# Rows of an attention stage turned by VectorE in 32x32 blocks and written from SP's queue, in place of TensorE transposes

## The chip, the cores and the metric

The kernel runs on one core of a Trainium2 chip. The time is the device time of that core in microseconds, taken as the median of several executions. The profile is one further execution, recorded by the hardware profiler.

## The reference

A linear attention with decay, for 4 sequences (b), 8 heads, 768 positions and 64 features per head, feeds a mixture of 8 experts. Cut to what matters:

```python
for b in range(nb):                      # blocks of positions, state carried on
    intra = (q_b @ k_b^T * Dmask) @ v_b  # Dmask = lam ** (i - j), lower triangle
    inter = (q_b * lam ** (i + 1)) @ kv_state
    out_b = intra + inter
    kv_state = lam ** block * kv_state + (k_b * lam ** (block - 1 - i))^T @ v_b
x = out as (4, 768, 512)                 # heads side by side
logits = x @ w_gate                      # 8 experts
e = argmax(logits), or the expert of the token before if sigmoid(x @ w_local) >= 0.5
out = softmax(logits)[e] * (relu(x @ w1[e]) @ w2[e])
```

Everything is in float32. Which tokens an expert gets is known only at run time.

## The kernel before

**Stages.** The kernel has an attention stage, a routing calculation woven into it, and an expert stage. The attention stage has 24 steps (`NS`), one for each block of 128 positions (`c`, 6 of them) of each sequence (`b`, 4 of them); `ORDER` goes through the four sequences first. The expert stage gathers rows of tokens from a DRAM tensor `x_dram` (3072 rows of 512 features), turns them, multiplies them with the weights of one expert at a time, and scatters the results.

**One step.** Step `s` takes an input tile `inp` of 1 MB: q and k with features on the partitions, v and k with positions on the partitions, each 128 x 512. TensorE computes the scores of the step to come (`scores`, line 200 or 208), the part that comes from the state (`from_state`, 235), the mixing of the values by the scores (`mix`, 248), the update of the state (`update`, 262) and the rows of the step before (`rows_of`, 272). VectorE multiplies the scores with the decay mask (212, two instructions) and adds to the state (265). ScalarE copies the result from PSUM to `xc` (251), decays the state (239) and copies the turned rows (277). GpSimd multiplies q and k with powers of lambda (`prepare`, 177 and 180), three steps ahead.

**The result `xc`.** It has features on the partitions: `xc[p, d, b, i]` is feature 128 d + p of position i. The gating product (`gates`, 286, every fourth step) reads it so. The expert stage needs whole rows of tokens in DRAM. So `rows_of(s)` turns the four 128 x 128 pieces with TensorE into one PSUM bank, ScalarE copies the bank into a tile `xn` (four buffers), and one DMA from ScalarE's queue writes 128 rows of 2 KB to `x_dram`; the last three of these writes go from SP's queue.

**Scores.** For steps in the list `WIDE` (3, 4 and 5) the scores are computed in 8 products with 128 keys each (line 200). In all other steps the keys are taken in halves of 64, in 16 products (line 208), and where a half lies behind all its first queries, those queries are left out.

**Order and queues.** In the attention stage the order on TensorE, VectorE, SP and GpSimd is the order of the program (`manual_schedule`); ScalarE's is chosen by the scheduler. SP's queue carries the input loads: the load of step s + 5 is issued at the top of step s, into one of six buffers, and waits until step s - 1 has been done with its buffer. Weights of the first two experts follow from step 16 on, on the same queue. Routing work stands in a table `extras` by step: constants (`constants_2` to `constants_6`, steps 6 to 10) are converted from integers or from float32 to what the routing needs, by VectorE, and from step 9 on the routing itself runs there.

**Weights.** `w1` is reordered on the host (`swapped`) so that its rows stand in the order of the features in `x_dram`.

Of the kernel before, what the change touches and what calls it, by code (L numbers as in the profile page):

```python
# [8 lines left out]
F32 = mybir.dt.float32  # L9
# [14 lines left out]
P = 128  # L24
B, H, S, DH = 4, 8, 768, 64
A = H // 2
DM = H * DH
E, F = 8, 1024
DT, FT = DM // P, F // P
N = B * S  # L30
NT = N // P
NC = S // P
ORDER = [(b, c) for c in range(NC) for b in range(B)]
# [5 lines left out]
PARTS = [(0, 8), (8, NA), (NA, NT)]  # L39
LOADS = 6  # L40
QUARTERS = [16, 17, 18, 19]
WIDE = [3, 4, 5]
WARM = 10
KA = -(-(NA * P - E * (P - 1)) // P)

# [2 lines left out]
HP = P // 2  # L48
QP = P // 4
# [5 lines left out]
G = G2 + E  # L55
# [9 lines left out]
def kernel(  # L65
# [9 lines left out]
    nc = tc.nc  # L75
# [7 lines left out]
    x_dram = dram.tile([N, DM], F32, name="x_dram")  # L83
# [18 lines left out]
    ident = const.tile([P, P], F32, name="ident")  # L102
# [4 lines left out]
    pg = ctx.enter_context(tc.tile_pool(name="pg", bufs=1, space=PSUM))  # L107
    x_ctx = ExitStack()
    load = x_ctx.enter_context(tc.tile_pool(name="load", bufs=LOADS))
    att = x_ctx.enter_context(tc.tile_pool(name="att", bufs=2))  # L110
# [11 lines left out]
    def piece(k):  # L122
        return spare[:, A * P * k:A * P * k + A * P]
# [35 lines left out]
    NS = len(ORDER)  # L159
# [4 lines left out]
    xc = att.tile([P, A, B, P], F32, name="xc", bufs=1)  # L164
# [21 lines left out]
    def scores(s):  # L186
# [8 lines left out]

        if s in WIDE:
            for a in range(A):
                for u in range(2):
                    rows = slice(DH * u, DH * u + DH)
                    nc.tensor.matmul(ps[u][:, a], lhsT=kt[rows, a], rhs=qt[rows, a],  # L200
                                     start=True, stop=True, skip_group_check=True)
        for a in range(A if s not in WIDE else 0):
            for j in range(2):
# [63 lines left out]
                nc.vector.tensor_copy(kv, pk)  # L267

    def rows_of(s):
        px = pg.tile([P, DM], F32, name="pk1")  # L270
        for a in range(A):
            nc.tensor.transpose(px[:, P * a:P * a + P], xc[:, a, ORDER[s][0]], ident)  # L272
        if s + 1 < NS:
            xn = att.tile([P, DM], F32, name="xn", bufs=4)
        else:
            xn = xlast
        nc.scalar.copy(xn, px)


        queue = nc.scalar if s + 3 < NS else nc.sync  # L280
        queue.dma_start(out=x_dram[P * s:P * s + P, :], in_=xn)

    def gates(k):

# [18 lines left out]
    count = const.tile([P, G + 1], F32, name="count")  # L303
    countb = const.tile([P, P], BF16, name="countb")
    whole = const.tile([P, G + 1], F32, name="whole")
    identb = const.tile([P, P], BF16, name="identb")
    onesb = const.tile([P, P], BF16, name="onesb")
    beforeb = const.tile([P, P], BF16, name="beforeb")
    dupb = const.tile([P, P], BF16, name="dupb")
    upper = const.tile([P, 1], F32, name="upper")  # L310
    dupq = const.tile([P, P], BF16, name="dupq")
# [4 lines left out]
    parts = route.tile([P, NT, 5], BF16, name="parts")  # L316
    ints = [piece(5 + i).bitcast(I32) for i in range(2)]
# [12 lines left out]
            nc.gpsimd.memset(t[:, :, 0:1], 0.0)  # L330

    def constants_2():
        nc.vector.tensor_copy(count, ints[0][:, :G + 1])
        nc.vector.tensor_copy(whole, ints[0][:, P:P + G + 1])
        nc.vector.tensor_copy(identb, ident)
        nc.vector.tensor_scalar(down, count[:, :E], -1.0, float(E), ALU.mult, ALU.add)

    def constants_3():
        nc.vector.tensor_copy(countb, ints[0][:, :P])

    def constants_4():
        nc.vector.tensor_copy(beforeb, ints[1][:, P:2 * P].bitcast(F32))
        nc.vector.tensor_copy(parts[:, :, 0], whole[:, 1:NT + 1])
        nc.vector.tensor_copy(parts[:, :, 1], ints[0][:, 2 * P:2 * P + NT])

    def constants_5():
        for half in range(2):
            nc.vector.tensor_copy(dupb[:, HP * half:HP * half + HP], ident[:, :HP])
        nc.vector.tensor_reduce(upper, ident[:, HP:], axis=AX.X, op=ALU.add)

    def constants_6():
        for k in range(4):
            nc.vector.tensor_copy(dupq[:, QP * k:QP * k + QP], ident[:, :QP])
        row = ints[0][:, 2 * P:2 * P + 1]
        nc.vector.tensor_scalar(row, row, P - QP, None, ALU.bitwise_and)
        nc.vector.tensor_scalar(fourth, row, 1.0 / QP, None, ALU.mult)
# [342 lines left out]
    xlast = moe.tile([P, DM], F32, name="xlast", bufs=1)  # L699
# [66 lines left out]
    def number(k, n):  # L766
# [3 lines left out]

    extras = {
        (6, 1): constants_2, (7, 1): constants_3, (8, 1): constants_4, (9, 1): constants_5, (10, 1): constants_6,
        (9, 0): lambda: fresh_experts(0), (10, 0): lambda: along_sequences(0), (11, 0): lambda: experts_of(0),
        (12, 0): lambda: ranks(0), (13, 0): lambda: fresh_experts(1), (14, 0): lambda: (along_sequences(1), masks(0)),
# [10 lines left out]
    with tc.manual_schedule(engines={PE, DVE, SP, POOL}):  # L785
# [16 lines left out]
        for s in range(NS):  # L802
# [4 lines left out]
            if s in QUARTERS:  # L807
                j = QUARTERS.index(s)
# [23 lines left out]
            if s == 1:  # L832
                query_powers(1)
                prepare(4)
                rows_of(0)
# [4 lines left out]
            if s > 1:  # L840
                rows_of(s - 1)
# [34 lines left out]
        moved(xtt[1], xq, (0, 1))  # L876
        hidden(0, 0, 0)
        rows_of(NS - 1)
        weights(1)
        gates(NC - 1)  # L880
# [452 lines left out]
```

## Time and profile before

| | |
|---|---|
| runs | 453.72 us median of 3 (451.68 to 459.57) |
| profiled execution | 449.21 us, span 447.5 us |
| granted TensorE clock | 0.995 |
| busy in the span | TensorE 433.0 us, VectorE 278.4, ScalarE 202.0, GpSimd 109.2 |
| attention stage | to about 103 us |
| four row transposes of a step | 0.59 us on the chain |
| `xn` copy, ScalarE | 586 ns each |
| 32x32 transposes of 128 x 512 on VectorE (expert stage) | 700 ns each |
| row write, issue to landing | 7.4 us (median of 21 DMAs, 256 KB each) |
| input load, issue to landing | 8.8 us (median of 15 DMAs, 1 MB each) |

A line of the chain of waits gives a start, a length and what ran; the numbers behind x are instructions. A line of the table of stages gives the stretch, its length, and then the busy time and the instructions of TensorE, its weight loads, VectorE, ScalarE and GpSimd, the granted clock, the busy share of the 16 DMA engines and GB/s. A line of the waits gives who waited for whom, the sum, how often, and the longest. A line of the DMA queues gives packets, MB and the share of 16 engines' time; a line of DMA issues gives the size and the median time from issue to landing.

### The profile page before, as it was taken

The numbers are of one execution on the slowest core, as the hardware profiler recorded it, in microseconds if no ns is written. First come the engines' busy times: TensorE is split into PE (matmuls) and PEld (weight loads), VectorE is DVE, ScalarE is ACT, GpSimd is POOL, SyncE is SP. The second block draws the span as 40 slices with busy tenths as digits, with TensorE's granted clock in tenths as the row PEclk, the third lists the DMA queues.
The fourth block names the chain that finished last, engine by engine and source line by source line (L and its number), as shares of the span: only waits on it lengthen the run. The fifth ranks groups of instructions, "written<-read, shape, count | busy, mean of one in ns | idle before, by whom it ended". The sixth has DMA issues, their size and how long they took to land.

```text
span 447.5 us, 10529 instructions
## 1 busy us (share of the span) xinstructions
PE 433.0 (97%) x4202; PEld 359.3 (80%) x4202; DVE 278.4 (62%) x562; ACT 202.0 (45%) x594; POOL 109.2 (24%) x120
## 2 busy tenths in 40 slices
PE   7999999999999999999999999999999999999993
PEld 6877877768667866979686999667899999898982
DVE  5546867881419949866473796100487888878661
ACT  2355656546453205553434447451445455556110
POOL 4476656231100041204120301210102011020101
PEclk9999999999999999999999999999999999999997
DMA  8999989988899889999995699997153838380101
GB/s 267 409 420 392 323 305 320 354 305 325 275 403 365 325 277 378 398 395 404 394 399 214 180 403 372 346 368 254 41 212 107 313 97 287 140 280 4 53 3 51
DMA packets 42575, 124.85 MB, mean 279 GB/s; under 512 B 3148, under 2 KB 3148, under 8 KB 40592
## 3 DMA queue, kind: packets, MB, share of 16 engines
q1 hardware_dynamic: 34976, 104.62, 64.0%
q0 software_dynamic: 4368, 13.90, 8.8%
q10 hardware_dynamic: 3168, 5.51, 3.3%
q8 instruction: 37, 0.61, 0.5%
q14 instruction: 26, 0.21, 0.1%
HBM read 124.02 MB, written 12.91 MB: 306 GB/s over the span
## 4 chain that ended last, share of the span: by engine, by line
PE 82%; DMA 7%; issue 6%; DVE 3%; POOLq 0%; POOL 0%
PE ps L731 13%; PE pk L737 12%; PE ps L956 12%; PE pk L961 11%; DMA out_dram<-y,sidxp 6%; PE po L248 6%; PE po L956 5%; PE pl L961 4%; PE ps L208 4%; PE pk L272 3%; PE po L235 2%; PE pk L262 2%; PE pr L1117 2%; PE pr L1095 2%; PE pl L286 1%
## 5 line engine op out<-in xcount | busy, mean ns | idle before, releaser
L731 PEld LDWEIGHTS ps<-xt,w 128*128 128x128 f32 x512 | 58.2, 192 | 3.0 <-issue 2.3
L731 PE MATMUL ps<-xt,w 128*128 128x128 f32 x512 | 59.1, 276 | 0.3 <-DVE xt L713 0.3
L737 PE MATMUL pk<-w,h 128*128 128x512 f32 x128 | 56.5, 593 | 0.0
L737 PEld LDWEIGHTS pk<-w,h 128*128 128x128 f32 x128 | 23.6, 190 | 26.3 <-issue 25.6
L746 POOL DMA_INDIRECT out_dram<-y,sidx x14 | 14.0, 1002 | 105.8 <-DVE y L763 46.5
L212 DVE TENSOR_TENSOR sm<-ps,mask 128x512 f32<-128x512 f32 x46 | 29.6, 685 | 16.1 <-PE ps L208 6.6
L703 POOL DMA_INDIRECT xg<-x_dram,gidx x25 | 25.8, 1032 | 55.2 <-DVE lg L717 24.6
L724 ACT COPY xp<-xlast 32x128 f32<-32x128 f32 x128 | 37.8, 295 | 1.7
L733 ACT ACTIVATE h<-ps 128x512 f32<-128x512 f32 x16 | 9.6, 597 | 57.6 <-PE ps L731 57.6
L724 ACT COPY xp<-lg 32x128 f32<-32x128 f32 x112 | 33.0, 295 | 2.6
L763 DVE TENSOR_SCALAR y<-pk,gate 128x512 f32<-128x512 f32 x8 | 6.0, 745 | 42.1 <-PE pk L737 40.0
L956 PEld LDWEIGHTS ps<-xp,w 128*128 128x128 f32 x256 | 30.5, 192 | 1.7 <-issue 1.3
L177 POOL TENSOR_TENSOR qd<-inp,lamq 128x512 f32<-128x512 f32 x20 | 25.6, 1278 | 25.1 <-PE po L235 15.8
L956 PE MATMUL ps<-xp,w 128*128 128x128 f32 x256 | 31.3, 275 | 0.0
L956 PE MATMUL ps<-xs,s 128*128 128x128 f32 x256 | 31.2, 275 | 0.0
L248 PE MATMUL po<-sm,inp 128*64 128x128 f32 x384 | 28.1, 280 | 2.5 <-DVE sm L212 1.4
L961 PE MATMUL pk<-w,h 128*128 128x256 f32 x128 | 30.5, 381 | 0.0
L961 PE MATMUL pk<-s,hsum 128*128 128x256 f32 x128 | 30.3, 380 | 0.0
L956 PEld LDWEIGHTS ps<-xs,s 128*128 128x128 f32 x256 | 29.9, 192 | 0.0
L248 PEld LDWEIGHTS po<-sm,inp 128*64 128x64 f32 x384 | 21.3, 136 | 10.2 <-issue 7.7
L961 PEld LDWEIGHTS pk<-s,hsum 128*128 128x128 f32 x128 | 23.9, 190 | 3.3 <-DVE s L1044 0.2
L961 PEld LDWEIGHTS pk<-w,h 128*128 128x128 f32 x128 | 23.5, 190 | 3.4 <-issue 0.6
(280 smaller groups left out, 793.9 us busy)
## 6 DMA issues: line engine op xcount, KB each, us to landing
w<-in_w_dram SPq DMA_DIRECT2D x43, 2048.0 KB, 11.8
inp<-in_qkv_dram SPq DMA_DIRECT2D x15, 1024.0 KB, 8.8
x_dram<-xn ACTq DMA_DIRECT2D x21, 256.0 KB, 7.4
inp<-in_qkv_dram SPq DMA_DIRECT2D x10, 512.0 KB, 7.9
inp<-in_qkv_dram SPq DMA_DIRECT2D x4, 768.0 KB, 6.9
w<-in_w_dram SPq DMA_DIRECT2D x4, 512.0 KB, 9.3
x_dram<-xn SPq DMA_DIRECT2D x2, 256.0 KB, 8.6
xg<-x_dram,gidx POOLq DMA_INDIRECT x25, 6.3
```

Source lines behind the costliest of these rows:

```text
L177: nc.gpsimd.tensor_tensor(qd, x[:, 0].rearrange("p (a i) -> p a i", i=P), lamq, ALU.mult)
L208: nc.tensor.matmul(ps[u][half, a, first:], lhsT=kt[rows, a, half], rhs=qt[rows, a, first:], start=True, stop=True, skip_group_check=True)
L212: nc.vector.tensor_tensor(sm[:, u], ps[u], mask[:, u], ALU.mult)
L248: nc.tensor.matmul(head(a, u), lhsT=vn[:, a, u], rhs=sm[:, u, a], start=(not c and a < 2), stop=True, skip_group_check=True)
L272: nc.tensor.transpose(px[:, P * a:P * a + P], xc[:, a, ORDER[s][0]], ident)
L703: nc.gpsimd.indirect_dma_start(out=xg, out_offset=None, in_=x_dram[:n, :], in_offset=bass.IndirectOffsetOnAxis(ap=gidx[i][:, j:j + 1], axi ...
L724: copy(xt[QP * j:QP * j + QP, :, QP * k:QP * k + QP], blocks[QP * k:QP * k + QP, :, j])
L731: nc.tensor.matmul(ph[:, j], lhsT=w1t[w][:, d, P * f:P * f + P], rhs=xtt[i][:, d], start=(d == 0), stop=(d == DT - 1))
L737: nc.tensor.matmul(pys[i], lhsT=hq[f // 4, i][:, f % 4], rhs=w2t[w][:, f], start=(f == 0), stop=(f == FT - 1))
L746: apart(nc.gpsimd.indirect_dma_start(out=out, out_offset=bass.IndirectOffsetOnAxis(ap=sidx[i][:, j:j + 1], axis=0), in_=y, in_offset=None, ...
L956: nc.tensor.matmul(to[:, m], lhsT=a[:, k, P * m:P * m + P], rhs=b[:, k], start=(new and not m and not k), stop=(k == 1), skip_group_check= ...
L961: nc.tensor.matmul(to, lhsT=a[:, f], rhs=b[:, f], start=(new and not f), stop=(f == FT // 2 - 1), skip_group_check=True)
```

## The change

In 14 of the 24 steps (`BY_BLOCKS`: 0 to 10, 12, 14 and 22) `rows_of` uses one VectorE instruction that transposes every 32 x 32 block of the step's part of `xc`. Partition 32 j + r of the tile `xn` then holds, for position 32 i + r of the block (i from 0 to 3), the 128 features with (feature mod 128) from 32 j to 32 j + 31. Four DMAs from SP's queue, one for each i, write this to 32 rows each, in pieces of 128 features (512 bytes). In the other ten steps TensorE still turns the rows, and ScalarE's copy brings the features into the same new order. The order of the features in `x_dram` is now (j, d, c) instead of (d, j, c), and `w1` is reordered on the host to match.

Thirteen conversions of constants move from VectorE to ScalarE. Steps 8 and 11 join the steps with 128-key scores.

```diff
-WIDE = [3, 4, 5]
+WIDE = [3, 4, 5, 8, 11]
+BY_BLOCKS = [*range(11), 12, 14, 22]
...
     def rows_of(s):
-        px = pg.tile([P, DM], F32, name="pk1")
-        for a in range(A):
-            nc.tensor.transpose(px[:, P * a:P * a + P], xc[:, a, ORDER[s][0]], ident)
-        if s + 1 < NS:
-            xn = att.tile([P, DM], F32, name="xn", bufs=4)
+        b = ORDER[s][0]
+        xn = att.tile([P, DM], F32, name="xn", bufs=4) if s + 1 < NS else xlast
+        if s in BY_BLOCKS:
+            nc.vector.transpose(xn.rearrange("p (i d c) -> p i d c", i=4, c=QP),
+                                xc[:, :, b].rearrange("p d (i c) -> p i d c", c=QP))
+            for i in range(4):
+                rows = x_dram[P * s + QP * i:P * s + QP * i + QP, :]
+                nc.sync.dma_start(out=rows.rearrange("a (j m) -> j a m", j=4), in_=xn[:, P * i:P * i + P])
         else:
-            xn = xlast
-        nc.scalar.copy(xn, px)
-        queue = nc.scalar if s + 3 < NS else nc.sync
-        queue.dma_start(out=x_dram[P * s:P * s + P, :], in_=xn)
+            px = pg.tile([P, DM], F32, name="pk1")
+            for d in range(DT):
+                nc.tensor.transpose(px[:, P * d:P * d + P], xc[:, d, b], ident)
+            nc.scalar.copy(xn.rearrange("p (j d c) -> p j d c", j=4, c=QP), px.rearrange("p (d j c) -> p j d c", j=4, c=QP))
+            queue = nc.scalar if s + 3 < NS else nc.sync
+            queue.dma_start(out=x_dram[P * s:P * s + P, :], in_=xn)
...
     def constants_2():
-        nc.vector.tensor_copy(count, ints[0][:, :G + 1])
-        nc.vector.tensor_copy(whole, ints[0][:, P:P + G + 1])
-        nc.vector.tensor_copy(identb, ident)
+        nc.scalar.copy(count, ints[0][:, :G + 1])
+        nc.scalar.copy(whole, ints[0][:, P:P + G + 1])
+        nc.scalar.copy(identb, ident)
...
-        "w1": swapped(i["moe_w1"]),
+        "w1": swapped(i["moe_w1"]).reshape(E, DT, 4, QP, F).swapaxes(1, 2).reshape(E, DM, F),
```

The ten conversions of `constants_3` to `constants_6` change from `nc.vector.tensor_copy` to `nc.scalar.copy` in the same way.

## The prediction

> **What bounds the kernel now.** I read the busy slices of the page first, then the table of stages, then the chain that ended last inside the attention stage, and last the DMA part, because the change moves work between four engines and onto another DMA queue.
>
> ```profile
> PE   7999999999999999999999999999999999999993
> ...
> DMA  8999989988899889999995699997153838380101
> ...
> 14.40:74.10 59.70, 57.91 (x1208) 45.94 (x1203) 38.75 (x93) 33.54 (x103) 37.24 (x32) 1.00 0.98 362
> ```
>
> The last line is a stage of my choosing, from the row writes of step 0 to the mixing of step 16. TensorE is busy in 57.91 of 59.70 us, VectorE in 38.75, ScalarE in 33.54, GpSimd in 37.24. The 16 DMA engines are at 0.98 as well: two resources are full at once. That matters more than anything else here, since the change takes work from one of them and gives work to the other.
>
> ```profile
> 65.43 0.45 PE po L235 x16
> ...
> 66.03 1.02 PE po L248 x16
> 67.05 0.63 PE pk L262 x16
> 67.68 0.58 PE pk L272 x4
> 68.26 0.81 PE ps L208 x24
> ```
>
> This is one attention step in the chain of waits: state, mixing, state update, the four row transposes (0.58 to 0.60 us in every step), the scores of the next step. The chain stays on TensorE throughout, so the 0.59 us of L272 are on the path. In the same chain the wide scores of steps 3 to 5 read 1.09 us (L200) against 0.81 (L208).
>
> ```profile
> GB/s 396 410 373 370 428 390 430 455 419 378 403 455 391 455 414 398 464 419 391 414 419 437 423 423 396 410 439 426 407 371 387 373 353 339 244 312 319 341 360 305
> ...
> q1 hardware_dynamic: 2321, 11.97, 84.9%
> q10 hardware_dynamic: 1143, 2.09, 15.1%
> ...
> inp<-in_qkv_dram SPq DMA_DIRECT2D x9, 1024.0 KB, 9.2
> x_dram<-xn ACTq DMA_DIRECT2D x9, 256.0 KB, 8.7
> ```
>
> This is the DMA view of 14 to 50 us: q1 is SP's queue (the inputs), q10 ScalarE's (the rows). Together they fill 16 engines, at some 400 GB/s. After about 45 us the rate falls: the six input buffers are full, and SP waits for TensorE instead, as the waits of its queue say:
>
> ```profile
> SPq L170 <- PE pk L262: 59.5, 17, 4.8
> ```
>
> So TensorE bounds the attention stage, but the input stream has spare time only in its second half.
>
> **What the Trainium skill says.** (1) "DMA: Bandwidth & Descriptors", the section on why a DMA increments its semaphore by 16 (paragraph "How many engines"): a copy is split along the slowest dimension of both patterns, over the largest number k of engines, at most 16, that divides both sizes, and on the SP and ScalarE queues these are the lowest-numbered k. The present row write has 128 rows on both sides, so k = 16; the trace agrees, its completion records are 16 for each DMA of q10. The new write is seen in DRAM as "j a m", outermost size 4: k = 4, engines 0 to 3, each time. No DMA of this trace has such a shape. (2) The same page, "Issuing engines are not separate DMA queues": another issuing engine brings no bandwidth. The view above agrees, q1 and q10 share one total. (3) "VectorE: DVE Perf Modes", "The three transpose paths": VectorE turns 32x32 blocks only, which is why feature order changes. Its price here comes from the trace, 700 ns for 128x512.
>
> **The change part by part.** Times of the profiled execution: span 447.5 us, 449.21 with what lies around it; the median of the runs is 453.72, 1.0% above, and the difference that I find is put on that.
>
> *TensorE.* 14 of 24 steps lose four transposes: 14 x 0.59 = 8.3 us off its path. Steps 8 and 11 get the wide scores: 2 x (1.09 - 0.81) = 0.56 us added. Net -7.7 us if everything else keeps up.
>
> *ScalarE.* It loses 14 copies of 586 ns and 14 DMA issues of 0.33 us (12.8 us), and gets 13 constant casts. Bounds: at the 0.19 to 0.3 us that its small copies take now, 2.5 to 3.9 us; at VectorE's own time, 6.3 us. Both lie in its idle time (26 of 59.7 us), so I take zero; without cover they would cost at most the difference to what was removed, which is below zero. The ten copies that stay read PSUM in another order at the same element count: bounds 0 and +0.3 us each; they lie beside TensorE, so zero.
>
> *VectorE.* It loses the casts (6.3 us in 13 instructions) and gets 14 transposes. Bounds for the strided input: 0.70 us as for the plain ones in the trace, or double. Per step 2 x 0.65 (sm) + 0.42 (kv) + 0.70 = 2.4 us, against a TensorE step of about 3.5: hidden, at 0.70. At double, 3.1, still hidden save in steps 12, 14 and 22 beside the routing work, at most 2 us in all.
>
> *SP.* 56 issues of 0.33 us come to its queue, behind a wait for VectorE's transpose. What is queued behind them is the next input load. Before, that load left when the state update freed its buffer; now it leaves after kv 0.42 + transpose 0.70 + four issues 1.3 + hand-overs 0.3 = 2.7 us later. Who waits for it is GpSimd two steps later, then TensorE.
>
> *DMA engines 0 to 3.* A row write is 4 x 32 x 4 = 512 packets of 512 B. By k = 4 engines 0 to 3 get 128 each, per step. Price of one: the single-packet records of the trace have medians of 84 ns for 2048 B, 159 for 4096 and 309 for 8192, a line of 9 ns + 75 ns per 2048 B; at 512 B this estimates 28 ns. Bounds: bytes alone, 21 ns; a heavier small packet, 40 ns. I take 28: 128 x 28 = 3.6 us on each of four engines, where the old write was 8 x 85 ns = 0.7 us on each of sixteen. A 1 MB input load costs every engine 2.4 to 2.5 us (420 GB/s at best).
>
> So engines 0 to 3 need 2.45 + 3.6 = 6.0 us per step in steps 0 to 10, TensorE about 3.5. A load is complete only when its slowest engine is done, and writes and loads are in one ring in SP's order. The sum up to input 23, the last: 20 loads x 2.45 = 49.0; 4 loads of three quarters, 7.4; 13 row writes (0 to 10, 12, 14) x 3.58 = 46.5; two weight quarters ahead of it, 2.5; eight rows of ScalarE's queue x 0.7 = 5.6; start 1.5. That is 112.5 us, then 1.5 for completion and 1.3 for GpSimd's product: the mixing of step 23 starts at 115.3. Before, it started at 100.9, in the chain. Difference +14.4 us. The 7.7 us of TensorE are swallowed, as it now waits. The four xn buffers point the same way: step s cannot turn rows until the write of step s-4 has landed. After the attention stage everything is TensorE-bound as before (109 to 380 us, 10.00 busy in each 10), so the shift stays: 449.2 + 14 = 463 for such an execution, 453.7 + 14 = **468 us** as a median.
> With 21 ns the sum is 13 x 128 x 7 ns = 11.6 less, +3; with 40 ns 20 more, +34.
>
> **The rivals.**
> *A, not slower:* the input stream has room for the writes. Place: the row writes; mechanism: they are spread over all engines after all (then 32 x 28 = 0.9 us per engine and step, 3.4 with the load, within TensorE's 3.5). TensorE's saving counts: 453.7 - 7.7 = 446. It decides from about eight engines on (2.45 + 1.8 = 4.2 us, near the present step of 4.1). For it speaks that TensorE's chain has no wait for an input today; against it, the shape of the write and a stream that is full up to 45 us.
> *B, SP's order:* writes spread, but each buffer's turn grows by 2.7 us. A buffer turns about four times in 24 steps: 4 x 2.7 = 10.8 less 7.7, +3: 457. For it: GpSimd already waits 0.6 to 0.75 us for inputs at 25 to 37 us. Against: later the loads land far ahead.
> *C, dearer small packets:* at 40 ns, +34: 488. Nothing in the trace shows such a price.
> *D, VectorE the bound:* +2 at most, on top of A: 448. Counted with A.
> That the rows are not turned as said has no place in the profile: the work is exchanged one to one.
>
> **How the numbers follow.** Likeliest case 0.66, A with D 0.13, B 0.11, C 0.10. Faster by over 2% (9 us, about what a measurement of this kernel can tell from no change) needs A and a little more: 0.05. Within 2%: the rest of A 0.08, B 0.11, the cheap end of the likeliest 0.06: 0.25. Slower: 0.70. The likeliest case alone spans 457 to 482 (24 to 36 ns); the range 448 to 488 takes in B and the two packet bounds, and leaves out most of A (0.10) and the tail of C (0.07).
>
> **What would show it right or wrong.** Right: in the attention stage TensorE's busy time falls well below the stage's length; GpSimd and TensorE wait for inp DMAs; VectorE's transposes wait for the xn writes; the mean DMA share falls (twelve engines idle) while loads take over 15 us to land instead of 8.8; TensorE reaches its first hidden product (103.3 us now) near 117. Wrong: loads still land in about 9 us and that product starts before 100 (A); loads late by 2 to 3 us only (B); completion records of a row write number 64 for a step instead of 16, which would say k = 16.

## The result, and the profile after

The changed kernel takes 476.92 us (median of four, 476.07 to 478.64); the kernel before took 452.7 us beside it. One of that kernel's four executions was a slow one, of 459.57 us, and is left out of the ratio. The ratio is 1.056, with a 95% interval of 1.050 to 1.062: slower by 24 to 25 us, where 14 us were forecast. The profiled execution took 477.28 us, with a span of 475.4 us, 27.9 us above the one before.

The busy slices of the page and the line of SP's DMA queue:

```profile
PE   8977776698799999999999999999999999999993
...
PEclk9997787989999999999999999999999999999997
DMA  7976665779798999999999659999524747560101
...
q1 hardware_dynamic: 42224, 108.03, 62.5%
```

One slice is 11.9 us. In most of slices 3 to 11, up to about 130 us, TensorE has sixes, sevens and eights where it had nines, and nowhere later. In most of the same slices the mean DMA share is below that of the kernel before as well. Both resources that were full are now partly empty, so something narrower than "the DMA engines" holds. The table of stages, for the stretch that was shown of before (same columns):

```profile
14.40:74.10 59.70, 44.52 (x812) 36.34 (x813) 29.90 (x67) 19.43 (x65) 24.04 (x22) 0.86 0.69 232
```

TensorE is busy 44.5 us of 59.7 (57.9 before), and the 16 DMA engines 0.69 (0.98 before). The granted clock, 1.00 before, is 0.86. The waits of the changed kernel from 10 to 110 us (who <- for whom: sum, times, longest) say on what:

```profile
POOL qd L178 <- DMA inp<-in_qkv_dram: 50.2, 15, 5.3
ACT kv L240 <- PE po L236: 42.0, 16, 6.0
...
PE ps L209 <- DMA inp<-in_qkv_dram: 17.7, 9, 3.8
```

GpSimd and TensorE wait for inputs. SP's own timeline shows the rhythm (start, length, what, how many):

```profile
31.88 2.73 SPq L171 DMA_DIRECT2D inp<-in_qkv_dram  x1
34.71 2.95 SPq L278 DMA_DIRECT2D x_dram<-xn  x4
37.78 2.82 SPq L171 DMA_DIRECT2D inp<-in_qkv_dram  x1
40.70 3.98 SPq L278 DMA_DIRECT2D x_dram<-xn  x4
44.79 3.46 SPq L171 DMA_DIRECT2D inp<-in_qkv_dram  x1
```

One load and four row writes leave per step, and SP needs 5.6 to 7.0 us for them from 26 to 70 us, because the issues take long. (In the kernel before, the issue of a load on SP took 0.33 us, as that of a row write on ScalarE did.)

The packet records carry the cause. Each row DMA left 4 completion records (224 for 56 DMAs), as k = 4 wants. A 512 B packet took 27 ns in the median. The records don't name the engine of a packet. Counting the time of the 512 B packets on four engines and of all others on sixteen, the load of these four comes to between 9.7 and 11.9 us in every 10 us from 20 to 110 us: they are full, while the mean over sixteen is some 0.7. The DMA share from 14 to 50 us in slices of 0.9 us, first before the change, then after it:

```profile
DMA  9999999999999999999999999999999989799998
```

```profile
DMA  9999999963959952679962295993229799232293
```

After the change the share swings between nearly all and 2 to 3 tenths, which is about four engines of sixteen. So the twelve others don't run ahead with the next load while the row packets pass: from 59.0 to 61.5 us 299 packets of 512 B started and 6 of a load's 8 KB, in the 2 us before 15 and 81. SP's issue of the next load was held meanwhile (57.91 to 60.90).

The starts of the mixing give the course. The changed kernel is 2.5 us ahead at step 6 (29.88 us, 32.35 before). From step 7 to step 15 it takes 6.38 us a step (37.75 to 88.78), the kernel before 4.23 (35.69 to 69.56). Step 23 is reached at 125.2 us, 100.8 before. The first hidden product of the expert stage starts at 129.64, 103.27 before. The remaining difference of the spans, 27.9 against 26.4, is small.

### The profile page after: what moved, and what is told of

The parts are those of the page before. It is cut to its first block, busy times and chain, and to the rows that moved or that the text cites. A ratio compares the mean times of both kernels' runs of the same rounds, so it can differ in the third digit from the quotient of the medians.

```text
span 475.4 us, 10450 instructions
## 1 busy us (share of the span) xinstructions
PE 438.3 (92%) x4114; PEld 364.5 (77%) x4114; DVE 284.5 (60%) x563; ACT 195.6 (41%) x593; POOL 108.2 (23%) x120
## 4 chain that ended last, share of the span: by engine, by line
PE 67%; DMA 18%; issue 6%; DVE 4%; SPq 4%; ACT 0%; POOLq 0%; POOL 0%; DVEq 0%
PE ps L735 12%; PE pk L741 12%; PE ps L960 11%; DMA inp<-in_qkv_dram 10%; PE pk L965 10%; DMA out_dram<-y,sidxp 6%; PE po L960 5%; PE pl L965 4%; PE po L249 2%; PE pr L1121 2%; PE pr L1099 2%; SPq L278 2%; DMA xg<-x_dram,gidx 1%; PE ps L209 1%; DVE sm L213 1%
## 5 line engine op out<-in xcount | busy, mean ns | idle before, releaser
L735 PEld LDWEIGHTS ps<-xt,w 128*128 128x128 f32 x512 | 59.6, 196 | 3.5 <-issue 2.3
L735 PE MATMUL ps<-xt,w 128*128 128x128 f32 x512 | 60.5, 280 | 0.8 <-DVE xt L717 0.8
L213 DVE TENSOR_TENSOR sm<-ps,mask 128x512 f32<-128x512 f32 x46 | 29.5, 683 | 31.1 <-PE ps L209 22.2
L741 PEld LDWEIGHTS pk<-w,h 128*128 128x128 f32 x128 | 23.6, 190 | 26.3 <-issue 25.6
L178 POOL TENSOR_TENSOR qd<-inp,lamq 128x512 f32<-128x512 f32 x20 | 25.5, 1275 | 62.2 <-DMA inp<-in_qkv_dram 57.6
L209 PE MATMUL ps<-inp 64*64 64x128 f32 (+1 forms) x576 | 18.3, 266 | 17.8 <-DMA inp<-in_qkv_dram 17.7
L240 ACT ACTIVATE kv<-kv,lamq 128x64 f32<-128x64 f32 x64 | 17.0, 337 | 42.0 <-PE po L236 42.0
L249 PE MATMUL po<-sm,inp 128*64 128x128 f32 x384 | 32.0, 311 | 1.2 <-issue 0.7
L249 PEld LDWEIGHTS po<-sm,inp 128*64 128x64 f32 x384 | 24.9, 156 | 10.1 <-issue 7.2
L209 PEld LDWEIGHTS ps<-inp 64*64 64x64 f32 x576 | 15.3, 143 | 20.5 <-issue 14.9
```

What stands on the lines that cost most here:

```text
L178: nc.gpsimd.tensor_tensor(qd, x[:, 0].rearrange("p (a i) -> p a i", i=P), lamq, ALU.mult)
L209: nc.tensor.matmul(ps[u][half, a, first:], lhsT=kt[rows, a, half], rhs=qt[rows, a, first:], start=True, stop=True, skip_group_check=True)
L213: nc.vector.tensor_tensor(sm[:, u], ps[u], mask[:, u], ALU.mult)
L240: nc.scalar.mul(kv[:, a], kv[:, a], lamq[:, a, P - 1:P])
L249: nc.tensor.matmul(head(a, u), lhsT=vn[:, a, u], rhs=sm[:, u, a], start=(not c and a < 2), stop=True, skip_group_check=True)
L735: nc.tensor.matmul(ph[:, j], lhsT=w1t[w][:, d, P * f:P * f + P], rhs=xtt[i][:, d], start=(d == 0), stop=(d == DT - 1))
```

## The experiments

The theory after the result (T1): the four-engine writes fill engines 0 to 3 and so delay the inputs. Its main rival (T2): it is SP's queue, with five DMAs in a step where there was one, that delays them, whatever engines carry the packets.

**Sixteen engines in place of four.** The cut of the four DMAs is turned: each takes a group of 32 partitions and all 128 rows, with the 32 rows outermost, so that k = 16 (the trace has 16 completion records for each). Packets stay at 512 B, and the rows in DRAM are the same.

```diff
-            for i in range(4):
-                rows = x_dram[P * s + QP * i:P * s + QP * i + QP, :]
-                nc.sync.dma_start(out=rows.rearrange("a (j m) -> j a m", j=4), in_=xn[:, P * i:P * i + P])
+            for j in range(4):
+                rows = x_dram[P * s:P * s + P, P * j:P * j + P]
+                nc.sync.dma_start(out=rows.rearrange("(i r) m -> r i m", r=QP),
+                                  in_=xn[QP * j:QP * j + QP].rearrange("p (i m) -> p i m", i=4))
```

> The four row DMAs of a turned step are cut by feature group j instead of by position group i: each moves 32 partitions, with 32 rows as the outermost dimension on both sides. Same 512 packets of 512 B, same four DMAs, same queue and waits; only the number of engines is 16 instead of 4. Theory 1 (four engines carry the writes): the input stream has room again, TensorE's saving counts, 443 to 450 us, inputs land in about 9 us, 64 completion records per turned step. Theory 2 (five DMAs per step on SP's queue, each of which has to wait for the completion of the one eight issues before it, so that at most one or two inputs are under way): the loss mostly stays, 465 to 475 us. Theory 3 (small packets as such are dear): stays at about 475.

Measured: 456.38 us, 450.69 for the kernel before; ratio 1.012 (1.009 to 1.015). That lies between the ranges of the two: the number of engines accounts for some 20 us, and 6 us stay. The waits of SP's queue in this kernel, from 10 to 110 us:

```profile
SPq L278 <- DMA inp<-in_qkv_dram: 17.8, 13, 2.6
SPq L278 <- DMA x_dram<-xn: 9.9, 4, 6.0
```

L278 is the row write. It needs no input tile, and yet it waits for input loads. The built program tells why: the DMAs of the SP and ScalarE queues signal eight semaphores in turn, and each waits until the DMA eight places before it has landed. With two DMAs in a step that reaches four steps back, with five only 1.6. So T2 has a share too: five DMAs in a step make SP wait.

**The writes from ScalarE's queue**, cut as in the change, k = 4.

```diff
-                nc.sync.dma_start(out=rows.rearrange("a (j m) -> j a m", j=4), in_=xn[:, P * i:P * i + P])
+                nc.scalar.dma_start(out=rows.rearrange("a (j m) -> j a m", j=4), in_=xn[:, P * i:P * i + P])
```

> The four row DMAs of a turned step, cut as in the changed kernel, go from ScalarE's queue instead of SP's. Theory 1 (four engines carry the writes): engines 0 to 3 have the same work, so the time stays within 6 us of the changed kernel, 471 to 483 us, with ScalarE now held at its issues. If instead the order on SP's queue was the cost (loads issued behind waits for VectorE and behind four issues): 450 to 458 us.

Measured: 484.87 us, ratio 1.073 (1.065 to 1.081), 2 us above what T1 named and far from T2's. Taking the writes out of SP's order gains nothing. It is somewhat worse; ScalarE now stands at the issues and the work of a step stands behind it (waits from 10 to 110 us):

```profile
PE po L236 <- ACT xc L252: 27.2, 10, 5.6
ACT kv L240 <- DMA x_dram<-xn: 24.7, 5, 6.8
```

**The gather before the last input.** At the end of the stage GpSimd's products for step 23 stand ahead of its first gather, and wait for the late input. Here they follow it.

```diff
-            if s + 3 < NS and s != 1:
+            if s + 3 < NS and s not in (1, 20):
                 prepare(s + 3)
...
+            if s == 20:
+                prepare(s + 3)
```

> The changed kernel, but in step 20 GpSimd gathers the first rows before it multiplies the queries of step 23, not after. If the gather stood behind GpSimd's wait for the last input (121.7 us in the changed kernel, while the indices were there at 114.2), the first hidden product starts 4 to 6 us sooner, and the whole takes 471 to 473 us. If the gather waits for the DMA engines in any case: within 1 us of the changed kernel, 476 to 478.

Measured: 476.09 us, ratio 1.054 (1.047 to 1.062): not to be told from the changed kernel's 1.056. GpSimd's timeline, first the changed kernel, then this one:

```profile
120.23 1.28 POOL L178 TENSOR_TENSOR qd<-inp,lamq 128x512 f32<-128x512 f32 x1 [2.48 <-DMA inp<-in_qkv_dram]
121.67 1.21 POOL L707 DMA_INDIRECT xg<-x_dram,gidx  x1 [0.17 <-DVE kd L480]
...
129.13 1.00 POOL L707 DMA_INDIRECT xg<-x_dram,gidx  x1 [4.92 <-PE pr L716]
```

```profile
115.25 1.21 POOL L707 DMA_INDIRECT xg<-x_dram,gidx  x1 [0.17 <-DMA inp<-in_qkv_dram]
...
126.66 1.04 POOL L707 DMA_INDIRECT xg<-x_dram,gidx  x1 [7.59 <-PE pr L716]
```

The gather leaves 6.4 us sooner, but the next one, which waits for TensorE to turn the first, starts only 2.5 us sooner. Moving it to the front is worth at most that, and no gain is seen in the times.

**No turns by VectorE.** `BY_BLOCKS` is empty; the new feature order, the casts on ScalarE and the wide scores of steps 8 and 11 stay.

```diff
-BY_BLOCKS = [*range(11), 12, 14, 22]
+BY_BLOCKS = []
```

> No step is turned by VectorE; the casts on ScalarE, the five wide steps and the new feature order stay. If these parts are small, as the prediction has it (+0.6 us for the two wide steps, casts hidden): 451 to 455 us, within 1 us of the kernel before. If the casts held VectorE up on the path: 446 to 449. If the reordered PSUM copies are slow: 455 to 460.

Measured: 451.54 against 450.69 us, ratio 1.000 (0.998 to 1.003). These parts of the change, the strided copies of ScalarE among them, cost nothing together. All that was lost hangs on the turned rows and their writes.

**The place in SP's order, alone.** The kernel before, every row turned by TensorE, its one row DMA (k = 16) issued by SP in the 14 steps.

```diff
-        queue = nc.scalar if s + 3 < NS else nc.sync
+        queue = nc.sync if s in (*range(11), 12, 14, 22) else nc.scalar if s + 3 < NS else nc.sync
```

> The kernel before, but in the same 14 steps the row write, still one DMA of 128 rows of 2 KB, goes from SP's queue. It has the place in SP's order alone: the next input load stands behind a wait for ScalarE's copy of the row. The two DMAs per step stay. If that place costs nothing much, as eight DMAs still reach back four steps: 450 to 453 us. If the order on SP is what holds the inputs: 456 to 465.

Measured: ratio 0.999 (0.997 to 1.002). A row write ahead of each load on SP is free.

**Four DMAs instead of one, alone.** The kernel before, as in the last, but with the row write as four DMAs of 32 rows each, k = 16, packets of 2 KB.

```diff
+        if s in (*range(11), 12, 14, 22):
+            for i in range(4):
+                nc.sync.dma_start(out=x_dram[P * s + QP * i:P * s + QP * i + QP, :], in_=xn[QP * i:QP * i + QP])
+            return
```

> The kernel before, TensorE and ScalarE turning all rows, but in the same 14 steps the row write goes from SP's queue as four DMAs of 32 rows of 2 KB (k = 16). No VectorE turn, no small packets. Theory 2: inputs are held by the row DMAs, 458 to 468 us (the saving of 7.7 us is missing and the waits of the run with sixteen engines are there). If only shape and size of the packets count: 449 to 453.

Measured: 455.31 against 450.65 us, ratio 1.012 (1.009 to 1.015), below the span that T2 named but above nothing. SP's waits are those of the first experiment, though VectorE turns no row and no packet is small in it:

```profile
SPq L282 <- DMA inp<-in_qkv_dram: 17.3, 12, 2.5
SPq L282 <- DMA x_dram<-xn: 8.5, 3, 4.1
```

So the number of DMAs costs 5 us by itself. That is close to the 6 us that the first experiment left, but TensorE's transposes were gone there and are still here, so it isn't shown that nothing else was lost there.

**Four engines, alone.** The kernel before once more, one row DMA in a step, but with the DRAM rows taken four apart, so that k = 4. Packets are 2 KB; the rows of a block come to stand in another order in DRAM. It ran twice: with the DMA on ScalarE's queue, and on SP's as in the experiment on the place in SP's order.

```diff
-        queue.dma_start(out=x_dram[P * s:P * s + P, :], in_=xn)
+        rows = x_dram[P * s:P * s + P, :]
+        if s in (*range(11), 12, 14, 22):
+            rows = rows.rearrange("(a i) m -> i a m", i=4)
+        queue.dma_start(out=rows, in_=xn)
```

> The kernel before (TensorE and ScalarE turn all rows, one row DMA per step, from ScalarE's queue, 2 KB packets), but in the same 14 steps the DMA sees its 128 rows as 4 x 32, so that it runs on four engines. The rows of such a block land in another order in DRAM, so later stages compute on permuted rows; work and waits are the same. This is the engine count alone: no VectorE turn, no small packets, no further DMAs, no new place in SP's order. Theory 1 (engines 0 to 3 are the bound): 32 packets x 84 ns = 2.7 us of writes and 2.5 of the input per step are 5.2 us against TensorE's 4.1, so 453 to 462 us. If four engines hurt only together with the eight completions: 449 to 452.

> The kernel before, TensorE turning every row, one row DMA per step, issued from SP's queue in the 14 steps (as in the run that moved it to SP and cost nothing), but with the DRAM rows taken four apart, so that the outermost size is 4 and k = 4; the rows of a block stand in another order in DRAM, nothing else is changed. In the run that did the same from ScalarE's queue ScalarE itself stood at its issues and at the xn buffers and no input was late, so its 13 us may not be the inputs' price. T1 (the load of engines 0 to 3 delays the inputs): a 2 KB packet takes 84 ns, a row write 32 x 84 ns = 2.7 us on each of four engines, with a load's 2.45 us 5.1 us per step against the 4.1 of the kernel before; the sum up to input 23 is 13 x 2.7 + 49.0 + 7.4 + 2.5 + 5.6 + 1.5 = 101 us plus the start's 3 us, and GpSimd waits for inputs for over 15 us: 454 to 462 us where the kernel before takes 450.5, mixing of step 23 at 105 to 112 us (100.8 before). T2 (only ScalarE's being held counted there): 449 to 452 us, and no input late.

Measured: from ScalarE's queue 463.92 against 450.41 us, ratio 1.031 (1.025 to 1.036); from SP's 462.92 against 450.28, ratio 1.026 (1.019 to 1.032). The two pay in different places. From ScalarE's queue (waits from 10 to 110 us) ScalarE waits for the `xn` buffers, one issue stood 4.79 us, and SP waits for TensorE, as before the change:

```profile
ACT xn L278 <- DMA x_dram<-xn: 11.4, 5, 5.6
```

From SP's queue it is the input that is late, as in the changed kernel:

```profile
POOL qd L177 <- DMA inp<-in_qkv_dram: 46.2, 19, 4.3
...
PE ps L208 <- DMA inp<-in_qkv_dram: 12.2, 9, 2.4
```

GpSimd's wait for inputs was 7.5 us in the experiment on the place in SP's order, from which this one differs by k and the order of the rows alone; from the first hidden product on both take 344 to 345 us. So 12 us or so are the four engines'. One load shows them: of its 16 completion records twelve came from 56.0 to 56.3 us, and the last four from 64.2 to 64.6. The mixing starts of this run are 5.26 us apart from step 8 to 15 (2.7 + 2.45 = 5.15 by the sum, if a row write is 32 packets of 84 ns on each of four engines), and the median input load took 16.9 us from issue to landing. Step 23 came at 115.4 us, later than the 105 to 112 that were expected, and the medians of both runs lie 1 to 2 us above the ranges of T1.

**Pairs of steps.** Sixteen engines as above, and steps 0 to 9 turned in pairs into one tile of two steps, with one set of four DMAs of 128 KB for each pair.

```diff
...
+            if s % 2:
+                for j in range(4):
+                    rows = x_dram[P * s - P:P * s + P, P * j:P * j + P]
+                    nc.sync.dma_start(out=rows.rearrange("(i r) m -> r i m", r=QP),
+                                      in_=xnn[QP * j:QP * j + QP].rearrange("p h (i m) -> p (h i) m", i=4))
...
```

> As the run with sixteen engines, but steps 0 to 9 are turned into a tile for two steps, and one set of four DMAs (k = 16, 128 KB each) writes both: three DMAs per step on SP's queue instead of five. Packets, bytes and VectorE's work are the same. Theory 2 (each of SP's DMAs waits for the one eight issues before it, and the row DMAs thus hold the next input): the waits of the row DMAs for inputs (17.8 us in the run with sixteen engines) fall to under 5, and the time falls from 456 to 446 to 450 us. If the rest comes from small packets or from VectorE's place in the chain: 454 to 458.

Measured: 452.3 against 450.65 us, ratio 1.004 (1.002 to 1.007), between the two. Mixing of step 15 was reached at 64.6 us, 5 us ahead of the kernel before. Then SP stood at the single writes of steps 12 and 14:

```profile
SPq L293 <- DMA x_dram<-xn: 14.2, 2, 7.2
```

Here the eight semaphores bind across two queues: in the built program SP's single write waits for a place that a write of ScalarE's queue holds, which comes late there. So the next two kernels leave no single VectorE-turned step among ScalarE's.

**Only the pairs, ten steps; then sixteen.** `BY_BLOCKS` ends with the pairs.

```diff
-BY_BLOCKS = [*range(11), 12, 14, 22]
+BY_BLOCKS = [*range(10)]
```

> As the run in pairs, but only steps 0 to 9 are turned by VectorE; 10, 12, 14 and 22 go the old way. In the run in pairs the mixing of step 15 starts at 64.6 us (69.6 before), and then SP stands at the row DMAs of steps 12 and 14 until 73 and 78 us, and the lead is gone by step 18. If those single turned steps, mixed with ScalarE's row DMAs, are what takes the lead back, the lead of some 5 us stays: 444 to 448 us. If the lead is lost at the end in any case (routing on VectorE, weights, the gather): 450 to 453.

> Steps 0 to 15 are turned by VectorE, all in pairs; the rest go the old way. Two more steps leave TensorE than in the changed kernel (9.4 us instead of 8.3). If SP's completions are the only cost left: 444 to 448 us. If VectorE, with routing work from step 9 on, is late with turned rows or scores: 451 to 456.

Measured: with ten steps 446.79 against 449.96 us, ratio 0.994 (0.991 to 0.996); with sixteen 445.97, ratio 0.993 (0.990 to 0.995). Both beat the kernel before, by 3 and 4 us, and the changed one. The stage table of the second:

```profile
14.40:74.10 59.70, 55.16 (x1200) 43.96 (x1202) 48.18 (x103) 27.61 (x95) 38.94 (x33) 1.00 1.00 358
```

The DMA engines are at 1.00 again and the rate at 358 GB/s (362 before, 232 in the changed kernel). Mixing of step 23 starts at 96.2 us, 4.6 us ahead.

**Twenty-two steps in pairs.**

> Steps 0 to 21 are turned by VectorE, all in pairs on 16 engines. TensorE loses 13 us instead of 9.4. If TensorE is still the bound of the late steps: 441 to 445. If VectorE, which does the routing there, becomes it: 446 to 452.

Measured: 448.44 against 450.41 us, ratio 0.995 (0.993 to 0.997): not above what sixteen steps gave. More of TensorE's transposes removed brings nothing further. VectorE was already busy 48.18 of 59.7 us with sixteen, and the later steps share it with the routing. That this is the cause was not tried by itself.

## Why the prediction was right, and which terms were off

*The mechanism.* Right. The row writes run on four engines, those four are the bound, and the inputs come late. "DMA: Bandwidth & Descriptors" of the Trainium skill, in its section on why a DMA increments its semaphore by 16, gave k = 4 from the shape alone; the trace agrees (4 completion records for each DMA), and changing k, with the cut that it needs, in both directions moved the time by 20 us (k = 16 in the changed kernel) and by 12 us (k = 4 in the kernel before). That a load is done only with its slowest engine is seen in the last k = 4 run (four records 8 us behind the other twelve). In the changed kernel it is not: there the last record of a load came 0.6 to 3.2 us behind the twelfth, much as before the change, and the loads were held earlier, at their issue (2.5 us in the median).

*The packet price.* Right: 28 ns were taken from the line through larger packets, 27 measured. By the same prices the 512 B packets make each of four engines work 128 x 27 ns = 3.46 us per step, against 2.69 for 2 KB: 0.77 x 13 steps = 10 us more. With the 12 us of four engines that is an estimate of 22 us, close to the 20 that k = 16 gave back. The packet size was not changed by itself.

*The sum.* Too low by 10 us in the medians and by 12 in the traces, in these terms. The last packet of input 23 ended at 119.6 us instead of 112.5. Of these 7 us, 3 lie ahead of the first row write: its last packet ended at 25.5 us, against some 22.2 by the sum. The rest is the step, 6.4 us instead of 6.03, over some eleven steps. The completion took 0.5 us where 1.5 was allowed. From there to the mixing of step 23 took 5.1 us, where the sum has 1.3 for GpSimd's product: input 23 was not what this mixing waited for. TensorE was still at the mixing of step 21 when it landed (120.0 us), and from 111 us on waited for no input. The last part is the end of the stage: the first hidden product came 4.4 us after that mixing, 2.5 us before the change. There the prediction overlooked that GpSimd issues in order: the gather's indices were ready at 114.2, and its issue stood behind products waiting for the last inputs. TensorE was idle for 1.9 us for these rows. The third experiment moved the gather, and got back 2.5 us at the next gather, at most.

*SP's queue.* The step "SP" failed. It priced 56 issues at 0.33 us and a load that leaves 2.7 us later. Measured, the place in SP's order costs nothing (0.999), and the number of DMAs costs 5 us, because only eight DMAs of the two queues may be out. None of this is in the 20 us that k = 16 gave back, since the four DMAs stayed there. Whether the 0.4 us by which a step exceeded the sum come from this limit or from gaps on engines 0 to 3 themselves stays open.

*The rivals.* B had the right place, SP's queue, and the wrong mechanism. A would not have come true even with its premise: at k = 16 the changed kernel takes 456 us, not 446. C fell with the 27 ns. D was not tried by itself; VectorE was busy only 29.90 us of 59.70. The span of the likeliest case was summed wrongly: 24 to 36 ns give 461 to 481 us by the prediction's own 13 x 128 packets, not 457 to 482. The measured 476.92 lies in both.

*TensorE's 7.7 us.* Swallowed, as said. About half can be had once the writes are cheap: the pairs of ten and sixteen steps gained 3 and 4 us.

*Nothing for the casts, the strided copies and the wide steps.* Right (1.000). VectorE's strided transposes took 702 ns, as plain ones do.

*What would show it right.* Three signs came: TensorE's busy time, GpSimd's and TensorE's waits, the DMA share. The first hidden product was late, but at 129.6 instead of 117. Two signs did not come. VectorE's transposes never waited for an `xn` write (0.2 us idle before all of them): with steps of 6.4 us the write of four steps earlier had landed. And the loads were not long in flight: that of step 14 was issued from 64.64 us on and landed at 73.8. The delay was in SP, which issued each load later; the chain of waits there is SP's issues for 60.9 to 70.2 us, and then a load of 10.49 us. With one row DMA per step on SP (the last k = 4 run) the same delay was seen in flight, 16.9 us.

## What to carry to other kernels

Before a transfer is moved to another layout, work out from the outermost sizes of both its sides how many DMA engines will carry it: mean DMA share hides four full engines among sixteen, and a load that uses all of them is held by these four, at its issue or at its end. Ask next how many DMAs it is cut into, since where only a few may be under way at a time (eight here) a small DMA takes a place as a large one does. Work taken off the busiest engine pays only when what it is traded for is cheap on the resource that is full beside it; here two steps' rows in one set of 16-engine DMAs, for sixteen steps, turned a loss of 5.6% into a gain of 0.7%.

## What the runs showed of the hardware

The granted TensorE clock fell in the stage, to 0.77 from 30 to 60 us, although TensorE had less to do. "TensorE: Matmul & The Clock Gate" of the Trainium skill, in its section on HAM oscillation, describes this: the clock is taken back while TensorE waits for a DMA. The changed kernel agrees (0.86 in the table of stages): in its clock records up to 100 us, each of the six idle times of TensorE of 2.0 us or more, up to 3.8, has a stretch of 3.4 or 6.8 us at half clock that begins in it or within 2 us after it. It need not be a DMA that is waited for: in the k = 4 run from ScalarE's queue TensorE waited up to 3.3 us for ScalarE, and the clock was 0.86 in the same stretch. In the last k = 4 run, where TensorE was busy 50.00 us of the same 59.70 and idle for at most 1.6 us at a time until 73 us, it stayed at 1.00; an idle time of 2.4 us right after that was followed by half clock. But the length of a single wait doesn't decide alone: one of 1.5 us at 101 us of that run was followed by half clock too, one of 2.0 us in the first run in pairs was not. How much of the 24 us is due to the lower clock was not separated.

An issuing instruction is not cheap when the transfers ahead of it are slow: on SP a load's issue took 2.5 us in the median of 19 in the changed kernel (0.33 before), and up to 4.8 us in the last k = 4 run, and it delays whatever stands behind it on its engine. "DMA: Bandwidth & Descriptors", in its section on issuing engines, says that another issuing engine brings no bandwidth; the run with the writes on ScalarE's queue agrees (1.073), and shows that it can bring a new wait.
